# A new order of the steps of a one-core attention and long-convolution kernel on Trainium2

## The chip, the cores and the metric

The kernel runs on one core of one Trainium2 chip. The metric is device time in microseconds (us); the shown time of a kernel is the median of several executions. The engines are named as in the profile: PE (TensorE matmul) with PEld (its weight loads), DVE (VectorE), ACT (ScalarE), POOL (GpSimd) and SP (SyncE). Each engine works through its own instructions in program order and waits on semaphores for the others.

## The reference

```python
kv  = einsum('bhsd,bhse->bhde', k, v)           # (8, 8, 64, 64)
o   = einsum('bhsd,bhde->bhse', q, kv)          # (8, 8, 576, 64)
x   = o / sqrt(mean(o*o, -1) + 1e-6) * g_norm   # -> (8, 576, 512)
x1, x2, x3 = split(x @ w_proj, 3)               # each (8, 576, 512)
x2c = irfft(rfft(x2, n=576) * rfft(filter, n=576), n=576)   # along the sequence
out = (x1 * x2c * x3) @ w_out                   # (8, 576, 512), float32
```

Inputs are float32; the loads cast them to bf16.

## The kernel before

The eight batches (0 to 7) go one after the other through the same steps, and steps of two or three neighbouring batches are interleaved. The order of all 688 steps is written out by hand in one text, `ORDER`; a word `name.batch` calls the step of that name, and each call issues its instructions on their engines at once. So `ORDER` fixes the program of every engine, the queues of SP and POOL among them. A third field (`T0.0.20`) puts that many idle products (512 columns, line 100) on PE ahead of the step.

The steps that the text below speaks of, with their engine and line:

- Loads on POOL's queue: `Lq`, `Lk`, `Lv` (one batch of q, k, v; `a` and `b` are halves; line 121), `Lw1` to `Lw3` and `Lwo` (weights, line 130), `Lf` (the filter, line 294). q, k and v have two buffers each, so batch n+2 waits until batch n is used up. `Zi` and `Zd` make index tables and the identity on POOL, `Zp` clears a part of the folded filter on POOL (its tile lies where the angles of the tables lay).
- `Qt` (line 405) transposes q by a DMA on SP's queue for batches 2 to 7; `Qh` (line 409) is a tiny POOL copy that reads the result. For batches 0 and 1 `T0`, `T1` (PE) and `eTv`, `eTa` (DVE) do it.
- `K`, `Ka`, `Kb` (PE, line 380) and `eK` (ACT) make kv, `O01`, `O23` (PE, line 454) the attention output, `sq`, `ob` (ACT) or `ov` (DVE) read it, `R`, `rs` (PE line 461, ACT line 475) the norm, `x0`, `x1` (DVE, line 489) the normalised x of two head pairs each.
- `fd`, `fr`, `fa` (DVE, lines 500 to 514) fold x along the sequence; both operands of their instructions lie in SBUF, as those of `x0` and `x1`. `rrM`, `rrT`, `abM`, `abT` (PE, lines 530 to 550) multiply the folds with w2; ACT copies the results out (`err`, `eab`, `eT`).
- `F0`, `F1`, `F2` (PE) are the forward transform, `M0`, `M1` (DVE, line 602) the products with the filter's transform: PSUM to the float32 tile `tpw`, 97 or 128 rows of 2048. `A0`, `A1` (POOL, line 608) sum the halves of `tpw` into the bf16 tile `Y`; `Av` does the same on DVE. `M2` (DVE, line 617) needs no sum.
- `Ga`, `Gb` (PE, line 627) are the two gates, `x10` to `x13` (ACT) and `g0` to `g3` (DVE, line 635: one operand in PSUM, one in SBUF) read them.
- `Io`, `I` (PE, lines 654 and 655), `os` (ACT), `u`, `w`, `fin` (DVE) are the inverse transform and the gating; `U`, `ot` (PE line 750, ACT and SP) the last product and the store.
- `Tb0` to `Tb2`, `Ff0` to `Ff2`, `H0` to `H2` build the tables and the filter's transform once, at the start.

PSUM is four pairs of banks. `take` gives a step the pair that was freed longest ago in `ORDER`; PE then waits until the engine named by that freeing step has read it. The functions that the change touches, and what calls them:

Of the kernel before, what the change touches and what calls it, by code (L numbers as in the profile page):

```python
# [19 lines left out]
ORDER = """Z.0 Zi.0 Lg.0 Lkb.0 Zt.0 Lq.0 Lvb.0 Lva.0 An.0 Lka.0 Zd.0 Zf.0 Lf.0 Tg.0 Zp.0 T0.0.20 Act.0 eTv0.0 T1.0 Lw1.0 Kb.0  # L20
eKb.0 Tb2.0 eTv1.0 Tb1.0 Lq.1 Lw2.0 Tb0.0 O23.0 sq2.0 Ka.0 R2.0.1 sq3.0 eKa.0 ov2.0 O01.0 rs2.0 ov3.0 sq1.0 R3.0 ov1.0
sq0.0 R1.0.1 rs3.0 rs1.0 x1.0 R0.0 ov0.0 rs0.0 x0.0 Ff2.0 Ff0.0 fd0.0 Ff1.0 Ga0.0 fr0.0 fr1.0 Lw3.0 fa0.0 Ga1.0 x11.0
Lv.1 fd1.0 x10.0 H1.0 H0.0 rrM.0 Lk.1 fa1.0 T0.1 rrT.0 err.0 eTa0.1 H2.0 Gb1.0 HN0.0 HN1.0 abM.0 F0.0 Gb0.0 eab.0 g1.0
K.1 M0.0 T1.1 abT.0 Lk.2 g0.0 eK.1 O01.1 eTa1.1 eT.0 sq0.1 ob0.1 F2.0 F2t.0 M2.0 sq1.1 Ga2.0 Lv.2 Lq.2 x12.0 Gb2.0
ob1.1 R1.1 g2.0 rs1.1 F1.0 R0.1 F1t.0 O23.1 rs0.1 sq2.1 Ga3.0 ob2.1 sq3.1 M1.0 R2.1 rs2.1 x0.1 ob3.1 x13.0 Av1.0 A0.0
Gb3.0 g3.0 R3.1 rs3.1 Lq.3 Qt.2 K.2 eK.2 Io01.0 I01.0 x1.1 Ga1.1 fd.1 Ga0.1 os01.0 u01.0 x11.1 Io23.0 O01.2 fr.1 x10.1
os23.0 sq0.2 I23.0 sq1.2 rrM.1 Qh.2 ob0.2 u23.0 ob1.2 Qt.3 R0.2 fa.1 rs0.2 w.0 rrT.1 err.1 O23.2 fin.0 abM.1 sq2.2
ob2.2 F0.1 eab.1 sq3.2 abT.1 eT.1 Gb1.1 Gb0.1 ob3.2 F1.1 M0.1 g1.1 R2.2 F1t.1 Lv.3 g0.1 rs2.2 Lk.3 R3.2 Ga3.1 rs3.2
R1.2 x13.1 Lwo.0 K.3 Lk.4 rs1.2 M1.1 Gb3.1 A0.1 x1.2 F2.1 Lv.4 x0.2 eK.3 A1.1 O23.3 F2t.1 g3.1 sq3.3 sq2.3 M2.1 fd.2
fa.2 U0.0 Io01.1 ob3.3 ob2.3 os01.1 ot0.0 Ga2.1 I01.1 x12.1 Gb2.1 R3.3 Io23.1 u01.1 rs3.3 g2.1 os23.1 I23.1 O01.3  # L30
abM.2 Lq.4 u23.1 w.1 sq1.3 sq0.3 Qh.3 Lq.5 Ga0.2 fin.1 ob1.3 ob0.3 abT.2 eab.2 x10.2 Ga1.2 R1.3 eT.2 fr.2 R0.3 x11.2
Gb1.2 rs1.3 F1.2 R2.3 rs0.3 F1t.2 g1.2 rrM.2 rs2.3 F2.2 rrT.2 K.4 M1.2 Qt.4 Lk.6 F2t.2 U2.0 eK.4 Lv.6 Lk.5 Lv.5 err.2
x1.3 Ga3.2 x0.3 M2.2 O23.4 ot2.0 x13.2 F0.2 sq3.4 sq2.4 ob2.4 Lq.6 ob3.4 fr.3 U0.1 M0.2 Qt.5 Gb0.2 R2.4 g0.2 Gb3.2
ot0.1 rs2.4 A1.2 A0.2 R3.4 g3.2 rrM.3 rs3.4 Io01.2 rrT.3 I01.2 os01.2 err.3 I23.2 Ga2.2 Gb2.2 fd.3 x12.2 fa.3 u01.2
g2.2 Io23.2 os23.2 u23.2 abM.3 abT.3 U4.1 eab.3 Ga0.3 ot4.1 F1.3 eT.3 w.2 fin.2 x10.3 O01.4 sq1.4 ob1.4 Qh.4 F1t.3
M1.3 sq0.4 U2.1 Ga1.3 ob0.4 ot2.1 F0.3 K.5 x1.4 A1.3 x11.3 F2.3 Gb0.3 eK.5 F2t.3 M0.3 R0.4 g0.3 Ga2.3 rs0.4 x12.3 R1.4
Gb2.3 M2.3 O23.5 rs1.4 Gb1.3 g2.3 x0.4 sq3.5 A0.3 sq2.5 ob3.5 ob2.5 U0.2 Io01.3 I01.3 Qt.6 fd.4 g1.3 fa.4 Ga3.3 os01.3
Gb3.3 x13.3 u01.3 Io23.3 g3.3 fr.4 abT.4 ot0.2 O01.5 os23.3 I23.3 eT.4 sq0.5 ob0.5 u23.3 Lk.7 abM.4 sq1.5 K.6 ob1.5
w.3 Ga0.4 eab.4 F1.4 R2.5 eK.6 x10.4 F1t.4 rs2.5 R3.5 rs3.5 rrM.4 R0.5 rs0.5 F2.4 fin.3 M1.4 x1.5 rrT.4 F2t.4 err.4
Ga1.4 R1.5 Gb1.4 M2.4 x11.4 Lv.7 rs1.5 O23.6 g1.4 sq3.6 F0.4 U2.2 sq2.6 ob3.6 Qh.5 Ga3.4 M0.4 ob2.6 ot2.2 O01.6 x13.4  # L40
Gb3.4 sq1.6 x0.5 Gb0.4 ob1.6 A1.4 g3.4 sq0.6 R3.6 ob0.6 A0.4 rs3.6 g0.4 U4.3 Ga2.4 ot4.3 R2.6 Gb2.4 fr.5 x12.4 rs2.6
fd.5 Io01.4 R1.6 I01.4 g2.4 os01.4 rrM.5 Io23.4 rs1.6 rrT.5 u01.4 os23.4 err.5 K.7 x1.6 I23.4 R0.6 Zn.0 fa.5 u23.4
abM.5 abT.5 rs0.6 eK.7 eab.5 U2.3 Lq.7 F0.5 Ga0.5 Qt.7 ot2.3 w.4 F1.5 fin.4 eT.5 F2.5 x10.5 M0.5 A0.5 F1t.5 U0.4 x0.6
M1.5 ot0.4 F2t.5 M2.5 A1.5 U0.3 Gb0.5 ot0.3 O23.7 sq3.7 g0.5 Ga1.5 Gb1.5 ob3.7 x11.5 fd.6 Io01.5 Ga2.5 fa.6 sq2.7 g1.5
I01.5 ob2.7 Ga3.5 os01.5 Io23.5 fr.6 x12.5 x13.5 Gb3.5 u01.5 Gb2.5 I23.5 os23.5 g3.5 g2.5 abM.6 Ga0.6 u23.5 eab.6
x10.6 O01.7 sq0.7 abT.6 ob0.7 eT.6 sq1.7 w.5 rrM.6 ob1.7 F1.6 Qh.6 rrT.6 F2.6 F1t.6 fin.5 err.6 F2t.6 U0.5 M1.6 Ga1.6
A1.6 F0.6 ot0.5 R2.7 M2.6 R1.7 x11.6 rs2.7 Gb0.6 U4.5 rs1.7 M0.6 R0.7 Gb1.6 A0.6 ot4.5 g0.6 R3.7 rs0.7 Ga2.6 U2.4
rs3.7 g1.6 I01.6 x12.6 Io01.6 Gb2.6 ot2.4 x1.7 Ga3.6 x0.7 fr.7 os01.6 u01.6 g2.6 rrM.7 fd.7 fa.7 x13.6 Io23.6 I23.6
os23.6 Gb3.6 g3.6 rrT.7 Ga1.7 err.7 abM.7 x11.7 u23.6 eab.7 F0.7 Ga0.7 x10.7 abT.7 w.6 F1.7 M0.7 eT.7 fin.6 Gb0.7 g0.7
F1t.7 F2.7 Ga2.7 x12.7 A0.7 F2t.7 Gb1.7 M1.7 U2.5 Av1.7 Qh.7 M2.7 g1.7 U2.6 Gb2.7 vae0.6 Io01.7 vve1.6 I01.7 ot2.5  # L50
g2.7 dse0.6 Ga3.7 dge1.6 J3.7 os01.7 x13.7 uj3.7 J2.7 dge2.6 uj2.7 U0.6 Gb3.7 u01.7 w01.7 dae3.6 fin01.7 wo23.7 wm23.7
Vq0.7 ot0.6 U4a.7 g3.7 fo23.7 U4b.7 vau.7 fm23.7 dsu2.7 Vq2.7 Vp0.7 dgu1.7 vaq0.7 vvq1.7 dsu0.7 dgu3.7 Vp2.7 dgq1.7
dsq0.7 dsq2.7 vap0.7 daq3.7 vvp1.7 dgp3.7 dap1.7 dsp0.7 dgp2.7"""


@with_exitstack
def kernel(
# [249 lines left out]
    def fold_filter(a, ev):  # L307
        pp = take("ffp")
        for odd in range(2):
            for s in range(2):  # L310
# [2 lines left out]
        ev(out=tmp['ff'][:, a], in_=pp)
        free("ffp")

    @one
    def Ff2(b):
# [4 lines left out]
        for odd, ev in enumerate((vec.tensor_copy, act.copy)):
            ev(out=tmp['ff'][0:32, 2, odd], in_=pp[32 * odd:32 * odd + 32])
# [554 lines left out]
```

## Time and profile before

| | |
|---|---|
| median of 3 runs | 218.24 us (218.19 to 220.13) |
| profiled execution | 219.81 us |
| its span, first to last instruction | 218.0 us |
| mean granted TensorE clock | 0.987 |
| busy: PE, DVE, ACT, POOL | 200.0, 184.0, 147.4, 68.1 us |

The profiled execution took 1.8 us more than its span and 1.6 us more than the median. In the lists of instructions, the columns are the start in us from the span's begin, the duration in us, engine, line, operation, tiles, shapes and the count of merged instructions; in brackets stands the idle time of the engine just before, and what ended it. A merged row's duration runs from the first start to the last end. In the table by stretches, each engine has its busy us and its instruction count.

### The profile page before, as it was taken

The numbers are of one execution on the slowest core, as the hardware profiler recorded it, in microseconds if no ns is written. First come the engines' busy times: TensorE is split into PE (matmuls) and PEld (weight loads), VectorE is DVE, ScalarE is ACT, GpSimd is POOL, SyncE is SP. The second block draws the span as 40 slices with busy tenths as digits, with TensorE's granted clock in tenths as the row PEclk, the third lists the DMA queues.
The fourth block names the chain that finished last, engine by engine and source line by source line (L and its number), as shares of the span: only waits on it lengthen the run. The fifth ranks groups of instructions, "written<-read, shape, count | busy, mean of one in ns | idle before, by whom it ended". The sixth has DMA issues, their size and how long they took to land.

```text
span 218.0 us, 4583 instructions
## 1 busy us (share of the span) xinstructions
PE 200.0 (92%) x1825; PEld 123.2 (57%) x1848; DVE 184.0 (84%) x275; ACT 147.4 (68%) x232; POOL 68.1 (31%) x67
## 2 busy tenths in 40 slices
PE   4978899898999999599999999999999999999960
...
PEclk9999999999999999799999999999999999999998
...
GB/s 64 203 208 206 205 204 203 187 182 163 205 174 146 230 86 146 230 156 191 240 147 188 121 0 98 154 115 96 164 32 0 38 111 96 0 3 18 178 205 132
DMA packets 40810, 30.12 MB, mean 138 GB/s; under 512 B 15796, under 2 KB 36276, under 8 KB 40788
## 3 DMA queue, kind: packets, MB, share of 16 engines
...
q14 instruction: 8, 0.07, 0.1%
...
## 4 chain that ended last, share of the span: by engine, by line
PE 69%; DVE 15%; DMA 5%; issue 3%; ACT 3%; POOL 1%; POOLq 0%; DVEq 0%; ACTq 0%
PE ps L627 24%; PE ps L750 10%; PE ps L544 5%; DMA wp<-in_moe_w_proj_dram 5%; DVE tpw L602 4%; PE ps L654 4%; PE ps L530 3%; PE ps L550 3%; PE ps L461 3%; PE ps L380 2%; PE ps L537 2%; PE ps L454 2%; PE ps L763 1%; PE ps L569 1%; PE ps L576 1%
## 5 line engine op out<-in xcount | busy, mean ns | idle before, releaser
L627 PE MATMUL ps<-x,wp 128*128 128x288 bf16 x512 | 72.5, 288 | 2.9 <-DVE tpw L602 2.4
L608 POOL TENSOR_TENSOR Y<-tpw 97x1024 bf16<-97x1024 f32 (+1 forms) x14 | 36.9, 2638 | 100.9 <-DVE tpw L602 100.8
L627 PEld LDWEIGHTS <-wp 128*128 128x128 bf16 x512 | 48.9, 98 | 21.5 <-issue 6.0
L602 DVE TENSOR_TENSOR tpw<-ps,HH 97x2048 f32<-97x2048 f32 (+1 forms) x16 | 36.6, 2288 | 3.6 <-PE ps L583 1.9
L635 DVE TENSOR_TENSOR g<-ps,x 128x576 bf16<-128x576 f32 x32 | 24.0, 753 | 8.3 <-PE ps L627 6.5
L475 ACT ACTIVATE rstd<-ps,bias_eps 128x576 bf16<-128x576 f32 x32 | 23.1, 748 | 7.5 <-PE ps L461 7.5
L633 ACT CAST x<-ps 128x576 bf16<-128x576 f32 x32 | 20.5, 644 | 10.9 <-PE ps L627 10.4
L750 PE MATMUL ps<-wo,yg 128*128 128x512 bf16 x106 | 26.0, 379 | 0.6 <-DVE g L635 0.2
L554 ACT CAST x<-ps 128x1024 bf16<-128x1024 f32 (+1 forms) x24 | 21.0, 874 | 8.2 <-PE ps L544 5.2
L464 ACT ACTIVATE sq<-ps 128x576 bf16<-128x576 f32 x32 | 20.1, 657 | 1.8 <-PE ps L454 1.6
L471 ACT ACTIVATE o<-ps,g_col 128x576 bf16<-128x576 f32 x28 | 20.3, 753 | 0.0
L754 ACT COPY ot<-ps 128x1024 f32<-128x1024 f32 x13 | 13.2, 1018 | 7.9 <-PE ps L750 7.8
L750 PEld LDWEIGHTS <-yg 128*128 128x128 bf16 x112 | 10.7, 98 | 12.1 <-issue 0.5
L654 PE MATMUL ps<-IV,Y 128*128 128x192 bf16 x120 | 15.6, 246 | 0.0
L544 PE MATMUL ps<-wp,ab 128*128 128x512 bf16 x58 | 14.8, 379 | 0.4
L663 DVE TENSOR_TENSOR u<-ps,os 128x576 bf16<-128x576 f32 x15 | 11.3, 754 | 3.1 <-ACT os L658 1.5
L461 PE MATMUL ps<-sq,ind 128*128 128x288 bf16 x64 | 13.0, 291 | 0.9 <-DVE o L469 0.5
L658 ACT COPY os<-ps 128x576 f32<-128x576 f32 x15 | 9.6, 642 | 5.5 <-PE ps L655 3.8
L655 PE MATMUL ps<-IV,Y 97*128 97x96 bf16 x60 | 12.4, 207 | 0.0
L489 DVE TENSOR_TENSOR x<-o,rstd 128x1152 bf16<-128x1152 bf16 x16 | 11.8, 750 | 0.7 <-ACT rstd L475 0.6
L386 ACT CAST kvblk<-ps 64x256 bf16<-64x256 f32 (+2 forms) x25 | 8.8, 353 | 4.5 <-PE ps L380 4.3
L654 PEld LDWEIGHTS <-Y 128*128 128x128 bf16 x120 | 9.6, 98 | 3.3 <-issue 1.1
...
## 6 DMA issues: line engine op xcount, KB each, us to landing
...
qb<-in_q_dram POOLq DMA_DIRECT2D x8, 576.0 KB, 8.7
vb<-in_v_dram POOLq DMA_DIRECT2D x7, 576.0 KB, 10.7
kb<-in_k_dram POOLq DMA_DIRECT2D x7, 576.0 KB, 12.2
wp<-in_moe_w_proj_dram POOLq DMA_DIRECT2D x3, 512.0 KB, 11.4
...
```

The source lines that it names most:

```text
L464: act.activation(out=halves(sq()[:, j]), in_=tmp['o', b, j][:, :, 0:TH], func=AF.Square)
L471: act.activation(out=by_time(osb(), j), in_=i_, func=AF.Copy, scale=g_col)
L475: act.activation(out=by_time(rstd(), j), in_=by_row(tmp['r', b, j]), func=AF.Abs_reciprocal_sqrt, scale=1.0 / D, bias=bias_eps)
L544: nc.tensor.matmul(pp[:, h], abt()[:, j, 2 * h * P:(2 * h + 1) * P], w2(j), start=(j == 0), stop=(j == NDC - 1))
L554: act.copy(out=o_(), in_=tmp[key, b])
L602: vec.tensor_mul(out=t_[:n], in0=xp[:n].unsqueeze(1).to_broadcast([n, 2, 2, DM]), in1=two)
L608: op(out=Yt()[:n, 2 * g:2 * g + 2], in0=t_[:n, ::-1, 0], in1=t_[:n, ::-1, 1])
L627: nc.tensor.matmul(pp[:, h, 0:TH], w_, x[:, j, h * TH:(h + 1) * TH], start=(j == 0), stop=(j == NDC - 1))
L633: act.copy(out=x1, in_=pp[:, :, 0:TH])
L635: vec.tensor_mul(out=halves(g13t()[:, dc]), in0=pp[:, :, 0:TH], in1=x1)
L654: nc.tensor.matmul(pp[:, i, 0:SB], Y[:, 2 * g + h, cs], IV[:, 2 * g + h, 0:SB], start=(g == 1), stop=(g == 2))
L750: nc.tensor.matmul(pp[:, cc], ygt(b)[:, dc, b % 2 * 64 + c * P:b % 2 * 64 + (c + 1) * P], wo[:, dc], start=(dc == 0), stop=(dc == NDC - 1))
```

## The change

`ORDER` is a new sequence of the same 688 steps; no step is added or dropped. The idle products ahead of `T0.0` become 22 (from 20), the one ahead of `R1.0` goes, the one ahead of `R2.0` stays. The tile of the folded filter is made by whichever step comes first (`ffb`), which issues no other instruction.

POOL's queue at the start and up to batch 7's loads, before and after (from `ORDER`):

```text
before: Zi Lkb.0 Lq.0 Lvb.0 Lva.0 Lka.0 Zd Lf Zp Lw1 Lq.1 Lw2 Lw3 Lv.1 Lk.1 Lk.2 Lv.2 Lq.2 A0.0 Lq.3 Qh.2
  Lv.3 Lk.3 Lwo Lk.4 A0.1 Lv.4 A1.1 Lq.4 Qh.3 Lq.5 Lk.6 Lv.6 Lk.5 Lv.5 Lq.6 A1.2 A0.2 Qh.4 A1.3 A0.3 Lk.7
  Lv.7 Qh.5 A1.4 A0.4 Lq.7 A0.5 A1.5 Qh.6 A1.6 A0.6 A0.7 Qh.7
after:  Zi Zd Lq.0 Lkb.0 Lvb.0 Lva.0 Lka.0 Lf Lq.1 Lw1 Lw2 Zp Lw3 Lk.1 Lv.1 Lv.2 Lk.2 Lq.2 A0.0 Lq.3 Qh.2
  Lk.3 Lv.3 Lwo A0.1 Lq.4 Lk.4 A1.1 Lv.4 Qh.3 A1.2 Lk.5 Lk.6 A0.2 Lq.5 Lv.5 Qh.4 A1.3 Lv.6 A0.3 Lq.6 Qh.5
  A1.4 A0.4 Lq.7 Lv.7 Lk.7 A0.5 A1.5 Qh.6 A1.6 A0.6 A0.7 ... Qh.7
```

The diff, with `ORDER` cut to the places that matter:

```diff
-ORDER = """Z.0 Zi.0 Lg.0 Lkb.0 Zt.0 Lq.0 Lvb.0 Lva.0 An.0 Lka.0 Zd.0 Zf.0 Lf.0 Tg.0 Zp.0 T0.0.20 Act.0 eTv0.0 T1.0 Lw1.0 Kb.0
-eKb.0 Tb2.0 eTv1.0 Tb1.0 Lq.1 Lw2.0 Tb0.0 O23.0 sq2.0 Ka.0 R2.0.1 sq3.0 eKa.0 ov2.0 O01.0 rs2.0 ov3.0 sq1.0 R3.0 ov1.0
-sq0.0 R1.0.1 rs3.0 rs1.0 x1.0 R0.0 ov0.0 rs0.0 x0.0 Ff2.0 Ff0.0 fd0.0 Ff1.0 Ga0.0 fr0.0 fr1.0 Lw3.0 fa0.0 Ga1.0 x11.0
...
-Gb1.2 rs1.3 F1.2 R2.3 rs0.3 F1t.2 g1.2 rrM.2 rs2.3 F2.2 rrT.2 K.4 M1.2 Qt.4 Lk.6 F2t.2 U2.0 eK.4 Lv.6 Lk.5 Lv.5 err.2
-x1.3 Ga3.2 x0.3 M2.2 O23.4 ot2.0 x13.2 F0.2 sq3.4 sq2.4 ob2.4 Lq.6 ob3.4 fr.3 U0.1 M0.2 Qt.5 Gb0.2 R2.4 g0.2 Gb3.2
-ot0.1 rs2.4 A1.2 A0.2 R3.4 g3.2 rrM.3 rs3.4 Io01.2 rrT.3 I01.2 os01.2 err.3 I23.2 Ga2.2 Gb2.2 fd.3 x12.2 fa.3 u01.2
...
+ORDER = """Zi.0 Z.0 Zd.0 Lg.0 Zt.0 An.0 Tg.0 Lq.0 Lkb.0 Zf.0 Act.0 T0.0.22 eTv0.0 Lvb.0 T1.0 Lva.0 Lka.0 Kb.0 eTv1.0 eKb.0 Tb1.0
+Tb0.0 Lf.0 Lq.1 O23.0 Lw1.0 sq2.0 Ka.0 Lw2.0 R2.0.1 sq3.0 eKa.0 ov3.0 Zp.0 Lw3.0 rs2.0 R3.0 ov2.0 Lk.1 O01.0 rs3.0
+sq1.0 sq0.0 x1.0 ov1.0 ov0.0 Ff0.0 Ff2.0 R1.0 rs1.0 R0.0 rs0.0 x0.0 Ff1.0 Tb2.0 T1.1 T0.1 eTa1.1 Ga0.0 fr0.0 fr1.0
...
+eab.2 rrM.2 rs1.3 F1.2 R2.3 F1t.2 g1.2 rrT.2 rs2.3 F2.2 err.2 x0.3 Qh.3 K.4 Qt.4 eK.4 F2t.2 M1.2 A1.2 U2.0 x1.3 M2.2
+Ga3.2 O23.4 ot2.0 x13.2 sq3.4 fr.3 Lk.5 F0.2 U0.1 sq2.4 ob3.4 Gb3.2 ob2.4 Gb0.2 Lk.6 M0.2 A0.2 fd.3 ot0.1 rrM.3 R2.4
+rrT.3 g0.2 Ga2.2 g3.2 rs2.4 R3.4 err.3 Io01.2 x12.2 I01.2 os01.2 rs3.4 U4.1 Io23.2 fa.3 Gb2.2 u01.2 os23.2 I23.2 abM.3
+Lq.5 ot4.1 abT.3 g2.2 x1.4 u23.2 eab.3 w.2 Ga0.3 eT.3 F1.3 O01.4 F1t.3 x10.3 U2.1 Qt.5 sq1.4 ob1.4 sq0.4 M1.3 Lv.5
+Ga1.3 ob0.4 fin.2 ot2.1 F0.3 R0.4 x11.3 rs0.4 Qh.4 K.5 eK.5 F2.3 M0.3 A1.3 Gb0.3 R1.4 g0.3 F2t.3 M2.3 rs1.4 Ga2.3
+x12.3 Gb2.3 O23.5 g2.3 sq3.5 ob3.5 Gb1.3 x0.4 Lv.6 A0.3 Ga3.3 g1.3 Io01.3 sq2.5 Lq.6 ob2.5 os01.3 x13.3 I01.3 fd.4
...
+    def ffb():
+        if 'ff' not in tmp:
+            tmp['ff'] = work.tile([P, 3, 2, DM], BF16, name="ff", tag="tpw1")
+        return tmp['ff']
+
     @one
     def Zp(b):
-        tmp['ff'] = work.tile([P, 3, 2, DM], BF16, name="ff", tag="tpw1")
-        nc.gpsimd.memset(tmp['ff'][:, 2], 0.0)
+        nc.gpsimd.memset(ffb()[:, 2], 0.0)
...
-        ev(out=tmp['ff'][:, a], in_=pp)
+        ev(out=ffb()[:, a], in_=pp)
...
-        ff = tmp['ff']
+        ff = ffb()
```

More of the change, by code (lines that the diff above doesn't have):

```diff
@@ L17 @@
 MAGIC = 3.0 * (2.0 ** 22)
-ORDER = """Z.0 Zi.0 Lg.0 Lkb.0 Zt.0 Lq.0 Lvb.0 Lva.0 An.0 Lka.0 Zd.0 Zf.0 Lf.0 Tg.0 Zp.0 T0.0.20 Act.0 eTv0.0 T1.0 Lw1.0 Kb.0
-eKb.0 Tb2.0 eTv1.0 Tb1.0 Lq.1 Lw2.0 Tb0.0 O23.0 sq2.0 Ka.0 R2.0.1 sq3.0 eKa.0 ov2.0 O01.0 rs2.0 ov3.0 sq1.0 R3.0 ov1.0
-sq0.0 R1.0.1 rs3.0 rs1.0 x1.0 R0.0 ov0.0 rs0.0 x0.0 Ff2.0 Ff0.0 fd0.0 Ff1.0 Ga0.0 fr0.0 fr1.0 Lw3.0 fa0.0 Ga1.0 x11.0
-Lv.1 fd1.0 x10.0 H1.0 H0.0 rrM.0 Lk.1 fa1.0 T0.1 rrT.0 err.0 eTa0.1 H2.0 Gb1.0 HN0.0 HN1.0 abM.0 F0.0 Gb0.0 eab.0 g1.0
@@ L24 @@
[L24 to L28, printed above, removed]
@@ L29 @@
-R1.2 x13.1 Lwo.0 K.3 Lk.4 rs1.2 M1.1 Gb3.1 A0.1 x1.2 F2.1 Lv.4 x0.2 eK.3 A1.1 O23.3 F2t.1 g3.1 sq3.3 sq2.3 M2.1 fd.2
-fa.2 U0.0 Io01.1 ob3.3 ob2.3 os01.1 ot0.0 Ga2.1 I01.1 x12.1 Gb2.1 R3.3 Io23.1 u01.1 rs3.3 g2.1 os23.1 I23.1 O01.3
-abM.2 Lq.4 u23.1 w.1 sq1.3 sq0.3 Qh.3 Lq.5 Ga0.2 fin.1 ob1.3 ob0.3 abT.2 eab.2 x10.2 Ga1.2 R1.3 eT.2 fr.2 R0.3 x11.2
-Gb1.2 rs1.3 F1.2 R2.3 rs0.3 F1t.2 g1.2 rrM.2 rs2.3 F2.2 rrT.2 K.4 M1.2 Qt.4 Lk.6 F2t.2 U2.0 eK.4 Lv.6 Lk.5 Lv.5 err.2
-x1.3 Ga3.2 x0.3 M2.2 O23.4 ot2.0 x13.2 F0.2 sq3.4 sq2.4 ob2.4 Lq.6 ob3.4 fr.3 U0.1 M0.2 Qt.5 Gb0.2 R2.4 g0.2 Gb3.2
@@ L34 @@
-ot0.1 rs2.4 A1.2 A0.2 R3.4 g3.2 rrM.3 rs3.4 Io01.2 rrT.3 I01.2 os01.2 err.3 I23.2 Ga2.2 Gb2.2 fd.3 x12.2 fa.3 u01.2
[L35 to L53, printed above, removed]
+ORDER = """Zi.0 Z.0 Zd.0 Lg.0 Zt.0 An.0 Tg.0 Lq.0 Lkb.0 Zf.0 Act.0 T0.0.22 eTv0.0 Lvb.0 T1.0 Lva.0 Lka.0 Kb.0 eTv1.0 eKb.0 Tb1.0
@@ new lines @@
+Tb0.0 Lf.0 Lq.1 O23.0 Lw1.0 sq2.0 Ka.0 Lw2.0 R2.0.1 sq3.0 eKa.0 ov3.0 Zp.0 Lw3.0 rs2.0 R3.0 ov2.0 Lk.1 O01.0 rs3.0
+sq1.0 sq0.0 x1.0 ov1.0 ov0.0 Ff0.0 Ff2.0 R1.0 rs1.0 R0.0 rs0.0 x0.0 Ff1.0 Tb2.0 T1.1 T0.1 eTa1.1 Ga0.0 fr0.0 fr1.0
+x10.0 eTa0.1 H0.0 H1.0 rrM.0 HN0.0 H2.0 rrT.0 Gb0.0 err.0 Gb1.0 fd0.0 g0.0 Ga1.0 fd1.0 F0.0 Lv.1 Lv.2 fa0.0 fa1.0 Lk.2
+Ga2.0 Lq.2 HN1.0 x11.0 K.1 x12.0 g1.0 M0.0 abM.0 abT.0 eK.1 eab.0 O01.1 eT.0 F2.0 sq0.1 A0.0 F2t.0 Gb2.0 ob0.1 M2.0
+sq1.1 F1.0 Lq.3 R1.1 g2.0 ob1.1 F1t.0 R0.1 rs1.1 rs0.1 Qt.2 M1.0 O23.1 Av1.0 sq2.1 ob2.1 sq3.1 Ga3.0 Gb3.0 x13.0 R2.1
@@ new lines @@
+ob3.1 Io01.0 R3.1 g3.0 x0.1 I01.0 rs2.1 K.2 rs3.1 os01.0 x1.1 eK.2 Io23.0 u01.0 fr.1 Ga0.1 os23.0 Ga1.1 x10.1 O01.2
+x11.1 fd.1 sq0.2 sq1.2 I23.0 ob1.2 fa.1 ob0.2 Qt.3 rrM.1 rrT.1 Qh.2 u23.0 abT.1 R0.2 Lk.3 w.0 err.1 eT.1 O23.2 rs0.2
+F0.1 sq2.2 sq3.2 ob3.2 abM.1 ob2.2 M0.1 Lv.3 Gb1.1 eab.1 R3.2 fin.0 R2.2 rs3.2 rs2.2 Gb0.1 F1.1 g1.1 Lwo.0 g0.1 R1.2
+F1t.1 A0.1 Ga3.1 rs1.2 M1.1 K.3 Gb3.1 x13.1 x1.2 eK.3 F2.1 O23.3 g3.1 F2t.1 Lq.4 sq3.3 Lk.4 M2.1 A1.1 sq2.3 U0.0
+Io01.1 ob3.3 I01.1 x0.2 ob2.3 os01.1 ot0.0 Ga2.1 Io23.1 fd.2 x12.1 Ga1.2 u01.1 os23.1 fa.2 x11.2 I23.1 R3.3 Gb2.1
```

19 lines of the change are left out of this document (18 added, 1 removed).

## The prediction

> **What bounds the kernel now.** I read the page's slices first, then the table by stretches around the one odd slice, then the chain and the engines' lists there. From the page:
>
> ```profile
> PE   4978899898999999599999999999999999999960
> PEclk9999999999999999799999999999999999999998
> ```
>
> PE is full in nearly every slice after the start. One slice, the seventeenth (from about 87 us), is half empty, and the clock dips there. By stretches:
>
> ```profile
> core 0: us, PE busy (x) PEld busy (x) DVE busy (x) ACT busy (x) POOL busy (x), PEclk, DMA share, GB/s
> 46.00:84.40 38.40, 36.76 (x371) 23.04 (x373) 36.66 (x48) 31.72 (x54) 15.36 (x17) 1.00 1.07 170
> 84.40:89.50 5.10, 2.98 (x19) 1.73 (x18) 5.10 (x4) 3.54 (x6) 2.33 (x2) 1.00 1.20 205
> 89.64:93.05 3.41, 3.19 (x13) 1.83 (x13) 2.03 (x4) 0.74 (x1) 2.28 (x2) 0.50 1.26 213
> 93.05:198.70 105.65, 104.96 (x898) 65.58 (x910) 93.99 (x113) 70.62 (x108) 27.45 (x15) 1.00 0.53 100
> ```
>
> From 46 to 84.4 PE and DVE share the bound (1.6 and 1.7 us idle of 38.4). From 93 to 199 PE alone is the bound: 0.7 us idle of 105.65, so no order can win there more than that. Between lie 2.12 us of idle PE and 3.41 us at a granted clock of 0.50. The chain says what PE waited for:
>
> ```profile
> 84.43 2.40 issue
> 86.84 0.35 DVE rr L509
> 87.18 2.21 DVE tpw L602
> 89.44 1.92 PE ps L627 x8
> ```
>
> The gate on PE waits for `M0.2` to free its PSUM pair, `M0.2` waits in DVE's queue behind `fr.3`, and `fr.3` stands for 2.40 us in which no semaphore was missing. DVE, then POOL, then PE in that place:
>
> ```profile
> 77.81 2.29 DVE L602 TENSOR_TENSOR tpw<-ps,HH 128x2048 f32<-128x2048 f32 x1
> 80.02 1.42 DVE L489 TENSOR_TENSOR x<-o,rstd 128x1152 bf16<-128x1152 bf16 x2
> 81.36 1.22 DVE L617 TENSOR_TENSOR Y<-ps,HM 128x1024 bf16<-128x1024 f32 x1
> 82.49 0.55 DVE L505 TENSOR_TENSOR x<-x 128x768 bf16<-128x768 bf16 x1
> 83.07 0.56 DVE L507 TENSOR_TENSOR x<-x,x 128x768 bf16<-128x768 bf16 x1
> 83.67 3.52 DVE L509 TENSOR_TENSOR rr<-x 128x384 bf16<-128x384 bf16 x2
> 87.10 2.28 DVE L602 TENSOR_TENSOR tpw<-ps,HH 97x2048 f32<-97x2048 f32 x1
> ...
> 82.79 0.77 POOL L121 DMA_DIRECT2D vb<-in_v_dram  x1
> 83.55 0.77 POOL L121 DMA_DIRECT2D qb<-in_q_dram  x1
> 84.33 2.36 POOL L608 TENSOR_TENSOR Y<-tpw 128x1024 bf16<-128x1024 f32 x1
> ...
> 84.21 1.89 PE L750 MATMUL ps<-wo,yg 128*128 128x512 bf16 x8
> 85.93 1.14 PE L627 MATMUL ps<-x,wp 128*128 128x288 bf16 x8
> 86.91 0.41 PE L461 MATMUL ps<-sq,ind 128*128 128x288 bf16 x2
> 89.44 1.92 PE L627 MATMUL ps<-x,wp 128*128 128x288 bf16 x8 [2.12 <-DVE tpw L602]
> ...
> L509 DVE TENSOR_TENSOR rr<-x x18: 249/351/3245, 22.6 to 180.7; 128x384 bf16<-128x384 bf16 x14, 128x192 bf16<-128x192 bf16 x4
> ```
>
> The first half of line 509 takes 3.25 us against a median of 0.35: 2.9 us lost, and it ends (86.9) with POOL's sum (84.33 + 2.36 = 86.7). It began at 83.67, ahead of the sum but behind the issue of `Lq.6` (83.55), on whose heels the sum followed without a gap. Line 507 ran at its usual length beside the issue before that one, so an issue alone does not hold DVE. `A1.2` had stood ready since `M1.2` ended at 80.1, behind five issues.
>
> The Trainium skill, "SBUF — State Buffer", section "SBUF: two separate sides", has VectorE and GpSimd share one port pair as an exclusive lock, won by whichever starts first. The trace agrees that a two-input DVE operation and a sum exclude each other, but not on who wins: here the one that started 0.66 us earlier lost.
>
> **The change, part by part.** *The hold.* In the new queue `A1.2` stands behind `Qh.3` and ahead of `Lk.5` and `Lk.6`; `Lv.6`, `Lv.5`, `Lq.6` move far behind. So nothing of `fr.3` falls behind an issue with a ready sum. What comes instead is the sum itself, right behind `M1.2`. How that goes:
>
> ```profile
> 62.15 3.47 POOL L608 TENSOR_TENSOR Y<-tpw 128x1024 bf16<-128x1024 f32 x1 [0.42 <-DVE tpw L602]
> ...
> 61.98 1.42 DVE L489 TENSOR_TENSOR x<-o,rstd 128x1152 bf16<-128x1152 bf16 x2
> 63.32 0.75 DVE L635 TENSOR_TENSOR g<-ps,x 128x576 bf16<-128x576 f32 x1
> ```
>
> DVE's two-input operations that stand directly behind the product go first (the sum is 1.1 us longer than the 2.36 above), and operations with one input in PSUM run beside a sum. The new DVE order is `x0.3 M1.2 x1.3 M2.2 fr.3 M0.2`. By the durations above: `x0.3` (0.71) now precedes `M1.2`, which ends at 80.8; `x1.3` to 81.5; the sum 81.5 to 83.85; beside it `M2.2` to 82.7; `fr.3` is held 1.15 us, to 83.85, then needs 0.55 + 0.56 + 2 x 0.35 = 1.8 to 85.65, `M0.2` 2.29 to 87.9. On PE, `Gb3.2` and `Gb0.2` (0.98 each) now both stand behind `U0.1`, from 85.93 to 87.9, and only then comes `rrM.3`, whose pair `M0.2` frees. So PE's wait falls from 2.12 to about 0: **-2.1**. If the sum did not hold `fr.3`, nothing more would be won, since PE is busy till 87.9; if `fr.3` were held the full 2.4 us, 1.2 would be lost again.
>
> *The clock.* Half speed for 3.41 us, with PE busy 3.19 of it, costs 1.6 to 1.7 us. It begins 0.2 us after the wait's end; a wait gone takes it along: **-1.7**, or 0 if something else brought it.
>
> The Trainium skill, "TensorE: Matmul & The Clock Gate", Part 1, "HAM oscillation", warns of idle gaps above some 3.4 us. Here 2.12 us sufficed, so the row is worse than the page; taken strictly, the page would leave the dip to another cause and the sum at 2.1 less.
>
> *The start.* POOL makes the identity first and loads q before k; `Zp` moves behind `Lw2`; `q.1` is loaded ahead of `Lw1`, and `T1.1`, `T0.1` and `Tb2` move up before `Ga0.0`; PE's work up to `K.1` stays the same but for an `abM` against a `Ga2` and a `T1`.
>
> ```profile
> 10.00:15.00 5.00, 4.26 (x100) 3.33 (x96) 3.54 (x11) 4.93 (x11) 4.16 (x6) 1.00 1.22 218
> 15.00:20.00 5.00, 3.77 (x38) 1.79 (x39) 4.12 (x7) 4.71 (x9) 2.93 (x5) 1.00 1.22 196
> 20.00:25.00 5.00, 4.41 (x44) 2.46 (x38) 4.76 (x15) 3.46 (x5) 0.74 (x1) 1.00 1.26 207
> ...
> 21.51 0.58 ACT L323 CAST ff<-ps 32x512 bf16<-32x512 f32 x1 [1.74 <-DVE ff L323]
> 22.11 1.93 ACT L313 CAST ff<-ps 128x1024 bf16<-128x1024 f32 x2
> ```
>
> ACT bounds the stretch from 10 to 20 (4.93 and 4.71 of 5). Two more idle products cost 2 x 0.24 (eight of that width in 1.89), one fewer gives 0.24 back: +0.24. ACT now casts `Ff0` (0.97) and `Ff2` (0.58) ahead of `rs1` and `rs0`, so `x0.0` and the first gate come 1.5 us later; the q transposes that PE meets there (0.6 each) fill most of it. I take **+0.5** together. Bounds: PE idles 0.74 + 1.23 + 0.59 = 2.56 in these rows, the most that a better start can win; the other end is 1.5 + 0.24 = +1.7 without the filling. The value lies near the loss end, since ACT's row is the fuller one.
>
> *The loads.* They now come later.
>
> ```profile
> qb<-in_q_dram POOLq DMA_DIRECT2D x8, 576.0 KB, 8.7
> ...
> DMA to landing us min/median/max: 18.3/18.3/18.3
> ...
> 106.52 0.95 PE L380 MATMUL ps<-vb,kb 96*64 96x64 bf16 x48
> ...
> DMA to landing us min/median/max: 6.3/6.3/6.3
> ...
> 135.48 0.79 POOL L121 DMA_DIRECT2D qb<-in_q_dram  x1
> 149.18 0.38 PE L576 MATMUL ps<-x,FY 128*128 128x512 bf16 x1
> ```
>
> These are the size of a load, `Lv.5`'s time to landing, the start of `K.5`, then `Lq.7`'s time to landing and issue, and the end of `F1.5`. The times below are on the old clock, without the start's 0.5. `Lv.5` landed at 82.8 + 18.3 = 101.1, 5.4 us before its use. Now it waits behind `A0.2`, which follows `M0.2` (87.9), `fd.3` (0.95) and lasts 2.36: `Lq.5` at 91.2, `Lv.5` at 92.0. An uncontended load lands after 6.3 us, and one behind it 2.9 later (576 KB at 205 GB/s): 100.4; at the pace of the crowded one (four such behind each other, 18.3 / 4 = 4.6) 104. `K.5` would come at 106.5 - 3.8 + 0.4 (`R0.4` ahead) = 103.1: from 2.7 early to 0.9 late. `K.7` now stands behind `F1.5`, with one gate more and itself less ahead of it: 149.6 - 3.8 = 145.8. Its `Lk.7` is third behind `A0.4` (135.5 - 3.8 = 131.7) and lands at 131.7 + 6.3 = 138.0 plus twice 2.9 to 4.6, 143.8 to 147.2: 2.0 early to 1.4 late. I take 0 for both, at most +2.3.
>
> *The rest.* `Qh.7` moves to the last stores, into POOL's waits there. SP's `Qt.5` goes behind `ot0.1` and `ot4.1`, after `Lq.5`. Elsewhere the order shifts a step or two among neighbours with equal PE work; 0.7 us is the most to win after 93, 1.6 between 46 and 84.
>
> Sum: -2.1 - 1.7 + 0.5 = **-3.3**: from the profiled execution's 219.8 to 216.5, its span from 218.0 to 214.7. That execution lay 1.6 above the median of 218.24, so I take the difference to the median: **214.9**.
>
> **Rivals.** *Late loads.* The wait goes, but `K.5` or `K.7` waits for its load: for it speaks the slack, down from 5.4 us to about none, against it that the DMA engines are less crowded from 93 on (share 0.53). All of +2.3: 217.2.
>
> *Late loads with the clock: slower.* `K.5` waits for v.5, because `Lq.5`, two stores and `Qt.5` share the engines with it. A wait of 2.1 us was enough to halve the clock; from there a wait of L costs L + 1.7. It decides at L = 1.6 to 2.1, where the gain of 3.3 is used up. At twice the crowded pace, v.5 lands at 92.0 + 6.3 + 2 x 4.6 = 107.5, L = 4.4: 214.9 + 6.1 = 221.0.
>
> *The clock dip stays* for another cause: 218.24 - 2.1 + 0.5 = 216.6.
>
> *The hold only moves.* `Lv.6` now stands directly ahead of `A0.3`, with `A0.3` ready when it is issued: the same picture. DVE then has `g0.3 M2.3 g2.3` (0.75 + 1.22 + 0.75 = 2.7), all with an operand in PSUM, before `x0.4`; issue and sum last 0.77 + 2.36 = 3.1, so 0.4 is held if PSUM work passes, 3.1 if not. The 63.32 row speaks for passing. If not, 218.
>
> *More than that:* the start gains its 1 and the middle 1: 213.
>
> **How the numbers follow.** Forecast 214.9 with 0.58 (own range 213.8 to 216.0); late loads 0.16; the dip stays 0.06; the hold moves 0.07; slower 0.08; more 0.05. The range of 8 in 10 runs from 213.2 to 217.8: it leaves out the slower rival and the tails. One per cent is 2.2 us and about what a measurement of this kernel tells from no change: below 216.06 lie the forecast but for its upper edge, "more" and a part of the late loads, 0.64; within 1% the rest of these and the moved hold, 0.28; slower 0.08.
>
> **What would show it.** No line 509 above 0.6 us; `fr.3`'s first instruction about 1.1 us longer than its 0.55; no PE wait on line 602 near 88; a 9 in every slice of the granted clock but the last; `K.1` within 1 us of its place. Wrong it would be made by a PE wait at `K.5` or `K.7` on a load, by another two-input DVE operation that lasts over 2 us, or by a first gate after 24 us.

## The result, and the profile after

The changed kernel took **217.39 us** (median of 20 executions, 216.30 to 220.70), the kernel before beside it 219.57 us (20 executions, 218.19 to 221.12). The ratio is 0.9914 with a 95% interval of 0.9888 to 0.9940; it compares means, without the changed kernel's two executions of 220.03 and 220.70 us, which count as slow. So the change is 0.9% less: the interval excludes a ratio of 1, but the gain stays under the one per cent that the forecast took as what a measurement of this kernel tells from no change. The time lies in the range of the forecast and 2.5 us above its value. A later set of the changed kernel gave 218.30 us (12 executions) and a ratio of 0.9936 (0.9903 to 0.9970).

The median of before moves between sets (218.24, 218.37, 219.05, 219.57, 219.82 us) because its executions fall into two groups, called the lower and the upper below: 8 of the 20 lay at 218.19 to 218.31 us, 10 at 219.43 to 219.85. The profiled execution of before (219.81) is of the upper group, the median of 218.24 that the forecast started from is of the lower.

Of the changed kernel an execution of the later set is read (217.68 us, span 215.9), since the first profiled one (220.70, span 218.9) ran a part of its start at half clock, that is at a granted clock of 0.50; that one is shown for the start and for its wait at `K.5`. The page's slices:

```profile
PE   4978999999999999999699999999999999999960
PEclk9999999999999999999999999999999999999996
```

The half empty slice at 87 us and the dip of the clock (3.41 us at 0.50) are gone. A new notch, a 6, stands in the twentieth slice, from 102.6 us. By stretches (busy us of each engine, then granted clock, DMA share and GB/s):

```profile
core 0: us, PE busy (x) PEld busy (x) DVE busy (x) ACT busy (x) POOL busy (x), PEclk, DMA share, GB/s
84.40:89.50 5.10, 5.05 (x33) 2.85 (x33) 5.07 (x7) 2.99 (x5) 2.65 (x3) 1.00 1.04 160
89.64:93.05 3.41, 3.41 (x35) 2.68 (x33) 3.03 (x5) 2.85 (x5) 2.68 (x4) 1.00 1.20 247
93.05:102.60 9.55, 9.50 (x67) 5.32 (x66) 8.60 (x11) 7.13 (x11) 1.21 (x1) 1.00 1.14 198
102.60:106.40 3.80, 2.18 (x60) 1.71 (x60) 2.18 (x1) 1.87 (x5) 3.79 (x3) 1.00 1.02 158
106.40:196.60 90.20, 89.41 (x736) 55.58 (x747) 81.70 (x100) 60.23 (x91) 24.19 (x14) 1.00 0.50 100
```

PE, idle for 2.12 of the 5.10 us from 84.4 before, is idle for 0.05, and the 3.41 us behind it run at full clock. The new idle time, 1.62 us, stands between 102.6 and 106.4. DVE, then POOL, then PE around the place of the old hold:

```profile
78.51 2.29 DVE L606 TENSOR_TENSOR tpw<-ps,HH 128x2048 f32<-128x2048 f32 x1
80.72 0.75 DVE L493 TENSOR_TENSOR x<-o,rstd 128x1152 bf16<-128x1152 bf16 x1
81.39 1.22 DVE L621 TENSOR_TENSOR Y<-ps,HM 128x1024 bf16<-128x1024 f32 x1
82.52 1.59 DVE L509 TENSOR_TENSOR x<-x 128x768 bf16<-128x768 bf16 x1
84.14 0.56 DVE L511 TENSOR_TENSOR x<-x,x 128x768 bf16<-128x768 bf16 x1
84.73 0.63 DVE L513 TENSOR_TENSOR rr<-x 128x384 bf16<-128x384 bf16 x2
85.28 2.28 DVE L606 TENSOR_TENSOR tpw<-ps,HH 97x2048 f32<-97x2048 f32 x1
...
80.88 2.81 POOL L612 TENSOR_TENSOR Y<-tpw 128x1024 bf16<-128x1024 f32 x1 [13.57 <-DVE tpw L606]
83.63 1.56 POOL L121 DMA_DIRECT2D kb<-in_k_dram  x2
...
85.66 2.12 PE L631 MATMUL ps<-x,wp 128*128 128x288 bf16 x16
87.62 1.03 PE L534 MATMUL ps<-wp,rr 128*128 128x512 bf16 x3
```

(The changed file's lines are 4 higher: old 505, 507, 509 are now 509, 511, 513; old 602 and 608 are 606 and 612.) The sum runs behind `M1.2`. `x1.3`, which began 0.16 us ahead of it, keeps its 0.75 (the sum lasts 2.81 instead of 2.36); `M2.2` with its PSUM operand keeps 1.22; `fr.3`'s first fold, begun at 82.52, takes 1.59 instead of 0.55 and ends 0.4 after the sum. The long first half of the old line 509 is gone, `M0.2` ends at 87.56, and PE goes from the gates to `rrM.3` without a wait.

What came instead stands in the chain of waits:

```profile
90.58 0.79 POOL qb L121
91.37 12.72 DMA vb<-in_v_dram
104.09 0.14 issue
104.23 0.95 PE ps L384 x48
```

`K.5` waits for v.5, issued at 91.37 and landed 12.72 us later.

### The profile page after: what moved, and what is told of

It is laid out like the page before. It is cut to its first block, busy times and chain, and to the rows that moved or that the text cites. A ratio compares the mean times of both kernels' runs of the same rounds, so it can differ in the third digit from the quotient of the medians.

```text
span 218.9 us, 4602 instructions
## 1 busy us (share of the span) xinstructions
PE 202.4 (92%) x1849; PEld 122.5 (56%) x1849; DVE 182.8 (84%) x275; ACT 148.1 (68%) x232; POOL 70.8 (32%) x67
## 4 chain that ended last, share of the span: by engine, by line
PE 69%; DMA 12%; DVE 7%; ACT 5%; POOL 3%; issue 2%; POOLq 0%; DVEq 0%; ACTq 0%
PE ps L631 24%; PE ps L754 9%; DMA vb<-in_v_dram 6%; PE ps L548 6%; DMA fn<-in_moe_filter_fft_dram 6%; PE ps L658 4%; DVE tpw L606 3%; PE ps L465 3%; PE ps L554 2%; PE ps L309 2%; PE ps L384 2%; PE ps L534 2%; PE ps L458 2%; PE ps L580 1%; PE ps L793 1%
## 5 line engine op out<-in xcount | busy, mean ns | idle before, releaser
L612 POOL TENSOR_TENSOR Y<-tpw 97x1024 bf16<-97x1024 f32 (+1 forms) x14 | 38.8, 2770 | 112.4 <-DVE tpw L606 112.3
L631 PE MATMUL ps<-x,wp 128*128 128x288 bf16 x512 | 71.3, 286 | 0.8 <-ACT rstd L479 0.3
L637 ACT CAST x<-ps 128x576 bf16<-128x576 f32 x32 | 20.5, 644 | 10.6 <-PE ps L631 10.5
L558 ACT CAST x<-ps 128x1024 bf16<-128x1024 f32 (+1 forms) x24 | 20.4, 881 | 6.8 <-PE ps L548 3.3
L754 PEld LDWEIGHTS <-yg 128*128 128x128 bf16 x112 | 10.6, 98 | 11.6 <-issue 0.5
L621 DVE TENSOR_TENSOR Y<-ps,HM 128x1024 bf16<-128x1024 f32 x8 | 9.7, 1218 | 2.2 <-PE ps L598 2.2
```

The lines of the kernel that those rows point to most:

```text
L612: op(out=Yt()[:n, 2 * g:2 * g + 2], in0=t_[:n, ::-1, 0], in1=t_[:n, ::-1, 1])
L631: nc.tensor.matmul(pp[:, h, 0:TH], w_, x[:, j, h * TH:(h + 1) * TH], start=(j == 0), stop=(j == NDC - 1))
L637: act.copy(out=x1, in_=pp[:, :, 0:TH])
L754: nc.tensor.matmul(pp[:, cc], ygt(b)[:, dc, b % 2 * 64 + c * P:b % 2 * 64 + (c + 1) * P], wo[:, dc], start=(dc == 0), stop=(dc == NDC - 1))
```

## The experiments

Each edit is in `ORDER`; the lines of code stay those of the kernel it starts from. The two theories at the outset: the time before was lost to a sum directly behind an issue, and given back by a load that is now late; or the order gains nothing there and the difference between the two kernels is one of the clock.

**Before, with the sum behind `M1.2`.**

```diff
-M1.2 Qt.4 Lk.6 F2t.2 U2.0 eK.4 Lv.6 Lk.5 Lv.5 err.2 x1.3 Ga3.2 x0.3 ... ot0.1 rs2.4 A1.2 A0.2
+M1.2 A1.2 Qt.4 F2t.2 U2.0 eK.4 Lk.5 Lv.5 Lk.6 Lv.6 err.2 x1.3 Ga3.2 x0.3 ... ot0.1 rs2.4 A0.2
```

> The kernel before with A1.2 moved directly behind M1.2, ahead of the five loads (and k.5, v.5 issued ahead of k.6, v.6, so that K.5 does not wait for its load). Nothing else moves. If the hold from the issue on is what cost the time: no line-509 instruction of 3.2 us; instead the first fold of fr.3 (line 505) about 1.0 us longer than its 0.55; PE's 2.1 us wait for M0.2 down to 1.0 or less; granted clock 1.00 from 86 to 94; 2.5 to 3.8 us less than the kernel before. Rival (any sum costs DVE the same, wherever it stands): the wait on M0.2 stays at 2 us and the time within 0.5 us of before.

Measured: 217.57 us (217.48 to 217.68), ratio 0.9929 (0.9904 to 0.9954): 1.5 us less than before, where at least 2.5 was expected. DVE, then POOL in this kernel:

```profile
80.04 3.58 DVE L489 TENSOR_TENSOR x<-o,rstd 128x1152 bf16<-128x1152 bf16 x2
83.54 1.21 DVE L617 TENSOR_TENSOR Y<-ps,HM 128x1024 bf16<-128x1024 f32 x1
84.67 0.54 DVE L505 TENSOR_TENSOR x<-x 128x768 bf16<-128x768 bf16 x1
...
80.20 2.79 POOL L608 TENSOR_TENSOR Y<-tpw 128x1024 bf16<-128x1024 f32 x1 [12.95 <-DVE tpw L602]
82.95 0.79 POOL L121 DMA_DIRECT2D kb<-in_k_dram  x1
```

Line 509 is at its usual length, and the five issues from 82.95 on, with no sum behind them, hold nothing. But here two `x` follow the product, and the second, begun at 80.70, after the sum, is held until the sum ends: the pair takes 3.58 us instead of 1.42, and PE waits 1.3 us for `M2.2`. So the long operation is the sum's doing wherever it stands; the place decides which DVE step pays.

**The same, with `x0.3` ahead of `M1.2`**, as the changed kernel has it.

```diff
-K.4 M1.2 A1.2 ... x1.3 Ga3.2 x0.3 M2.2
+K.4 x0.3 M1.2 A1.2 ... x1.3 Ga3.2 M2.2
```

> The first experiment (the kernel before with A1.2 behind M1.2) with x0.3 moved ahead of M1.2 as well. If the sum's own lock is what is left there: no line-489 instruction of 2.9 us; the first fold of fr.3 lasts 1.6 instead of 0.55; PE's waits of 1.3 and 0.3 us there gone; 1.0 to 1.6 us less than that first experiment, about 216.2. Rival (PE is bound by something else there): within 0.4 us of it.

Measured: 216.74 us (216.19 to 218.70, six executions), ratio 0.9884 (0.9843 to 0.9925), 0.8 us less than the first experiment, where 1.0 to 1.6 was expected.

```profile
83.70 1.58 DVE L505 TENSOR_TENSOR x<-x 128x768 bf16<-128x768 bf16 x1
```

The held `x` is gone, and `fr.3`'s fold pays 1.03 us, as in the changed kernel. The profiled execution (217.65) also has a wait of 1.8 us for a q transposition near 49 us, which the edits don't touch. These two edits of before, without any other part of the new order, are at least as good as all of it.

**Before, with one issue less ahead of the sum.**

```diff
-sq3.4 sq2.4 ob2.4 Lq.6 ob3.4 fr.3 ... A1.2 A0.2
+sq3.4 sq2.4 ob2.4 ob3.4 fr.3 ... A1.2 A0.2 Lq.6
```

> The kernel before with Lq.6 moved behind A0.2, so that A1.2 stands directly behind Lv.5's issue (82.8 to 83.55). If the issue ahead of a ready sum already takes the ports: the instruction of line 507 that starts at 83.07, inside that issue, is the long one (2.8 to 2.9 us instead of 0.56) and line 509 is normal. Rival (whoever starts first has the ports): line 507 lasts 0.56, the sum begins late or is longer, and the first instruction of line 509 takes about 2.6 us.

Measured: 219.42 us (218.06 to 219.71), ratio 0.9982 (0.9946 to 1.0019). DVE, then POOL:

```profile
82.63 0.55 DVE L505 TENSOR_TENSOR x<-x 128x768 bf16<-128x768 bf16 x1
83.21 3.28 DVE L507 TENSOR_TENSOR x<-x,x 128x768 bf16<-128x768 bf16 x1
86.53 0.63 DVE L509 TENSOR_TENSOR rr<-x 128x384 bf16<-128x384 bf16 x2
...
82.92 0.77 POOL L121 DMA_DIRECT2D vb<-in_v_dram  x1
83.70 2.36 POOL L608 TENSOR_TENSOR Y<-tpw 128x1024 bf16<-128x1024 f32 x1
```

The sum now follows `Lv.5`, and the long operation moves one instruction forward: line 507 takes 3.28 us instead of 0.56, having begun 0.49 us ahead of the sum but 0.29 behind the issue; line 509 is normal. This is the hold as the prediction read it: from an issue with a ready sum directly behind it, to the sum's end. Whether the issue does it, or the sum takes the ports earlier than its recorded start, the rows don't tell.

The Trainium skill, "SBUF — State Buffer", section "SBUF: two separate sides", gives the lock to whichever engine starts first. `x1.3` above, begun 0.16 us ahead of a sum with no issue before it, agrees; this row, and the row of line 509 in the kernel before, don't: there an issue stands directly ahead of the sum.

**Before, with idle products in PE's wait**: they end no wait of DVE or POOL, they only keep PE busy.

```diff
-Qt.5 Gb0.2 R2.4 g0.2 Gb3.2
+Qt.5 Gb0.2 R2.4.8 g0.2 Gb3.2
```

> The kernel before with eight idle products (1.7 us of PE) ahead of R2.4, inside PE's 2.1 us wait for M0.2; the wait's end is unchanged. If the wait itself halves the clock for the 3.41 us behind it: granted clock 1.00 there and 1.5 to 1.7 us less. Rival (the dip has another cause): the 3.41 us at 0.50 stay and the time is within 0.3 us of before.

Measured: 218.34 us (218.10 to 218.78), ratio 0.9959 (0.9930 to 0.9988). The stretches, then PE:

```profile
84.40:89.50 5.10, 4.71 (x28) 2.47 (x26) 5.10 (x4) 3.16 (x6) 2.33 (x1) 1.00 1.21 211
89.64:93.05 3.41, 3.38 (x27) 1.93 (x26) 2.81 (x4) 1.70 (x4) 3.08 (x2) 1.00 1.25 211
...
86.95 1.89 PE L100 MATMUL ps<-kvblk,ind 128*128 128x512 bf16 x8
89.48 1.14 PE L627 MATMUL ps<-x,wp 128*128 128x288 bf16 x8 [0.39 <-DVE tpw L602]
```

The hold stays (line 509: 3.25 us) and PE is released at the same time, but the clock stays at 1.00 and all twelve executions lie at or near the lower group of before. So the idle 2.12 us brought the half clock, and the half clock is the 1.5 us between the groups. Which group an execution falls into changes with the same program: in the sets beside the experiments, 31 of 69 executions of before took less than 218.4 us, with a mean granted clock of 0.988 to 0.996, and 35 took 219.6 or more, with 0.980 to 0.988. The mean clock alone doesn't place an execution: in the first experiment, 0.982 and 0.995 went with 217.52 and 217.60 us.

**The changed kernel, with v.5 loaded earlier.**

```diff
-fr.3 Lk.5 F0.2 ... M1.3 Lv.5 Ga1.3
+fr.3 Lk.5 Lv.5 F0.2 ... M1.3 Ga1.3
```

> The kernel after with Lv.5 moved up from behind A0.2 and Lq.5 to directly behind Lk.5. If the late v.5 costs its whole wait: PE's 2.16 us wait before K.5 gone (v.5 lands before 101 us), 1.8 to 2.2 us less than after, that is 3.8 to 4.3 less than before. Rival (the wait only moves, to O23.5 for q.5's transposes, which then land later, or to DVE): less than 1 us won against after.

Measured: 224.23 us (223.77 to 226.30, six executions), ratio 1.0242 (1.0194 to 1.0290): 2.4% more than before. `K.5` no longer waits, but `O23.5` waits for the q transposition. The issue of `Lq.5` (its time to landing), SP's `Qt.5`, and PE's `O23.5`:

```profile
L121 POOL DMA_DIRECT2D qb<-in_q_dram x1: 803/803/803, 93.1 to 93.1; - x1
DMA to landing us min/median/max: 13.2/13.2/13.2
...
106.44 3.04 SPq L409 DMA_TRANSPOSE qT<-qb  x1
...
115.78 0.69 PE L458 MATMUL ps<-qT,kvblk 64*64 64x288 bf16 x8 [5.95 <-DMA qT<-qb]
```

With v.5 ahead of it, q.5 lands at 106.3, 2.2 us later than in the first profiled execution of the changed kernel, where it was issued at the same time (93.0) and landed at 104.1. `Qt.5` can only start then, and lands after 9.3 us instead of 6.5. PE waits 5.95 us, and from 112.5 to 119.3 the granted clock is 0.50, half of that behind the wait. So a load that is moved ahead pushes back the next one. (This execution, 226.30 us, had a half clock in its start as well; the other five took 223.77 to 224.26.)

**The changed kernel, with q.5 and v.5 loaded earlier**, q.5 as before directly behind `Qh.3`.

```diff
-x0.3 Qh.3 K.4 ... fr.3 Lk.5 F0.2 ... abM.3 Lq.5 ot4.1 ... M1.3 Lv.5
+x0.3 Qh.3 Lq.5 K.4 ... fr.3 Lk.5 Lv.5 F0.2 ... abM.3 ot4.1 ... M1.3
```

> The kernel after with Lq.5 issued ahead of A1.2 (behind Qh.3) and Lv.5 directly behind Lk.5, so that neither stands behind A0.2. If the late loads of batch 5 are what eats the gain: no PE wait at K.5 (2.2 us in after) nor at O23.5 (6.0 us with v.5 alone moved), 1.5 to 2.3 us less than after. Rival (the DMA engines are the bound there, so that another load or transposes come late): within 0.7 us of after, with a PE wait of over 1 us on a DMA between 80 and 115 us.

Measured: **216.31 us** (216.04 to 216.50, six executions), ratio 0.9849 (0.9816 to 0.9881): the lowest median of all. PE waits nowhere more than 0.3 us between 20 and 200. The same kernel shows the place at which the hold might have moved, `Lv.6` directly ahead of `A0.3`, whose input `M0.3` is done at 105.10, just behind the issue's start; POOL, then DVE:

```profile
105.07 0.79 POOL L121 DMA_DIRECT2D vb<-in_v_dram  x1
105.87 2.36 POOL L612 TENSOR_TENSOR Y<-tpw 97x1024 bf16<-97x1024 f32 x1
...
105.21 0.76 DVE L639 TENSOR_TENSOR g<-ps,x 128x576 bf16<-128x576 f32 x1
105.88 1.21 DVE L621 TENSOR_TENSOR Y<-ps,HM 128x1024 bf16<-128x1024 f32 x1
```

Both operations, one begun behind the issue and one beside the sum, keep their usual length: work with an operand in PSUM passes. (In the changed kernel itself the product at 106.57 takes 0.76 beside that sum, which runs from 105.55 to 107.91.) No DVE operation with both operands in SBUF stands there, so the rows don't show what would happen to one.

**The changed kernel, with q.5 alone earlier**, to tell the queue's length from the time of `Lv.5`'s issue.

```diff
-x0.3 Qh.3 K.4 ... abM.3 Lq.5 ot4.1
+x0.3 Qh.3 Lq.5 K.4 ... abM.3 ot4.1
```

> The changed kernel with only Lq.5 moved, from ahead of Qt.5 to behind Qh.3; Lv.5 stays behind the q transposition's issue. Theory (K.5 waits because v.5 shares the engines with q.5, the output stores and Qt.5): v.5 lands after 6.3 to 10 us instead of 12.7 to 13.3, about 98 to 102, K.5 does not wait, and the time is that of the version with both moved, 216.3. Rival (v.5 is late because it is issued at 91 to 94, whatever stands ahead of it): K.5 waits 0.5 us or more and the time is 217 or above.

Measured: 216.36 us (216.01 to 216.72, six executions), ratio 0.9891 (0.9857 to 0.9926). `Lv.5`, then PE's `K.5`:

```profile
L121 POOL DMA_DIRECT2D vb<-in_v_dram x1: 803/803/803, 91.1 to 91.1; - x1
DMA to landing us min/median/max: 9.6/9.6/9.6
...
103.01 0.95 PE L384 MATMUL ps<-vb,kb 96*64 96x64 bf16 x48
```

`Lv.5` is issued at 91.1 as in the changed kernel (91.4), lands after 9.6 us instead of 12.7, and `K.5` doesn't wait. So what made it late is q.5 ahead of it, not the hour of its issue. One moved load recovers all that the two did (the times compare better than the ratios here: before had a median of 219.82 us beside the one and 218.37 beside the other).

**The changed kernel behind the start of before.** `ORDER` of before up to `K.1`, of after from there.

> The order of the kernel before up to K.1, and from there on the remaining steps in the order of after. If the new start loses time (filter landing 1.3 us later behind which q.1 and w1 are in flight, PE waiting on it, the clock halved from 17 to 24 us): 1 to 2.5 us less than after, no half clock between 10 and 30 us. Rival (the start is a draw and the half clock there is this one execution's): within 0.5 us of after.

Measured: 219.05 us (218.64 to 223.07), ratio 1.0007 (0.9979 to 1.0036): neither less than the changed kernel nor close to it. It settles little: `K.1` comes at 34.2, but the seam adds delays of its own (`Qt.2` lands after 10.5 us, PE waits 1.3 us for it, `K.4` comes at 81.6 instead of 79.0).

**Idle products ahead of the filter's first product**, in the changed kernel and in the version with q.5 and v.5 early.

```diff
-ov0.0 Ff0.0 Ff2.0
+ov0.0 Ff0.0.6 Ff2.0
```

In the changed kernel:

> The changed kernel with the same six idle products ahead of Ff0 and nothing else. Theory: its upper executions (219 to 220.7) go, what is left is 217.0 to 218.8 with the 1.6 to 2.2 us that K.5 waits for v.5; K.1 at 34.2 to 35.3 and no half clock before 25 us. Rival: the spread from 216.3 to 220.7 stays, because it comes from how late v.5 lands and not from the start.

In the version with both loads early:

> The version with q.5 and v.5 loaded early (216.31 us), and six idle products (0.22 us each) ahead of the first filter product Ff0 on PE, where two profiled executions of the changed kernel's start waited 1.36 and 1.58 us for the filter and then ran 6.83 us at half clock. Theory (the wait for the filter makes the start's half clock): no execution has half clock before 25 us, all lie within 0.5 us of each other, and K.1 starts at 34.2 to 35.3, so 216.3 to 217.4. Rival (the half clock in the start is a draw that no product prevents): the spread of the changed kernel, over 2 us, shows here too in a window before 25 us.

Measured: 217.69 us (216.64 to 219.19) and 216.82 us (216.35 to 217.42), ratios 0.9939 (0.9904 to 0.9973) and 0.9901 (0.9866 to 0.9936). Neither profiled execution has a half clock before 25 us. The products cost 0.5 us in the better version (`K.1` at 35.2 instead of 34.3), whose executions spread over 1.1 us, more than the 0.5 of the theory. In the changed kernel one of twelve executions lies above 219 us, against six of the 32 without the products: too few to tell theory and rival apart. The profiled one waits 0.6 us for v.5, where two others of this kernel waited 1.6 and 2.2, so a part of the spread comes from there.

## Why the prediction was right and wrong

**The hold: right.** The forecast had `fr.3` held by 1.15 us and PE's wait of 2.12 gone. The fold took 1.59 instead of 0.55 (+1.04), `M0.2` ended at 87.56 against the 87.9 of the forecast, and PE's wait went. (The sum began at 80.88, ahead of the 81.5 of the forecast, and was the longer for it.) The size is best read without the clock: from before without the dip (218.34 with idle products, 218.2 to 218.3 for its lower group) to the order without late loads (216.31 and 216.36) it is 2.0 us, all that the new order does elsewhere included; the forecast had 2.1.

**The clock: the right mechanism, booked twice.** The half clock came from the wait, as said, and went with it; 1.5 us against 1.7. But only about half of the executions have it. The step that failed is the last one of the sum, "I take the difference to the median". The sum of -3.3 was made against an execution with the dip and held there: 219.8 - 3.3 = 216.5, and the versions without late loads have 216.40 and 216.50 in their profiled executions. The 1.6 us between that execution and the median of 218.24 was this same dip, absent in the median. Taken off again, it made 214.9. The forecast's own rival, "the clock dip stays", had 216.6 by the sum that was due for that median, for another reason.

**The loads: the term that was mis-sized.** The forecast bounded `K.5` by 2.7 us early to 0.9 late and took 0. PE was there at 102.6 instead of 103.1, v.5 landed at 104.1, and the wait was 1.6 us in the execution shown and 2.2 in the first one. What was wrong is the 6.3 us to landing for q.5, the time of a load with none ahead of it: `Lk.6`, issued at 84.4, was still landing until 97.5 when `Lq.5` was issued at 90.6, so q.5 took 10.6 us (landed 101.2); v.5 came 2.9 us behind it, the spacing that the forecast had. The late bound of 104 fits the landing by luck, since the terms given beside it make 102.1 (91.2 + 6.3 + 4.6), ahead of PE. And the share of 0.53 that spoke against late loads is a mean over 105 us: in before it was 1.31 from 93.05 to 102.6 and 0.32 from 120 on. `K.7` waited for nothing.

The rival "late loads" had this wait, and its time of 217.2 is close to the measured one by luck: it added 2.3 us to a 214.9 that was 1.6 too low. Of the 2.5 us that the forecast missed, 1.6 are the dip counted twice. The other 0.9 fit `K.5`'s wait, which was 0.6 to 2.2 us in the profiled executions; the two versions without it took 1.0 less than the changed kernel (216.31 and 216.36 against 217.39). The other rival of a late v.5, in which its wait halves the clock again, did not come: the first profiled execution waited 2.16 us, and the 3.41 us behind that ran at 1.00.

```profile
107.23 0.95 PE L384 MATMUL ps<-vb,kb 96*64 96x64 bf16 x48 [2.16 <-DMA vb<-in_v_dram]
```

**The start: +0.5 forecast, 0.0 to +2.5 seen.** PE's `K.1` in before, then in the changed kernel's execution read above, then in its first profiled one with the wait for the filter and the stretch behind it:

```profile
34.22 0.95 PE L380 MATMUL ps<-vb,kb 96*64 96x64 bf16 x48
...
34.21 0.95 PE L384 MATMUL ps<-vb,kb 96*64 96x64 bf16 x48
...
17.98 0.62 PE L309 MATMUL ps<-fn,ident 96*32 96x512 bf16 x4 [1.36 <-DMA fn<-in_moe_filter_fft_dram]
36.69 0.95 PE L384 MATMUL ps<-vb,kb 96*64 96x64 bf16 x48
...
16.90:23.73 6.83, 5.75 (x44) 2.13 (x44) 3.07 (x5) 4.07 (x7) 1.54 (x2) 0.50 1.27 206
```

The later set was run to see whether the half clock is the rule of the new start (`K.1` at 36.7 again) or comes in some executions only (`K.1` at 34 to 35.5, 216.5 to 217.5 us): its profiled execution had full clock there and `K.1` at 34.21, but took 217.68 us. The casts of `Ff0` and `Ff2` ahead of the norms cost nothing in it. In the first profiled execution the first gate comes at 25.15, one of the forecast's own signs of being wrong, as PE's wait at `K.5` was. What the forecast didn't have: `Ff0` now stands some 2 us earlier on PE and needs the filter at about 16.5, where it lands between 16.4 and 18.1. Whether that wait brings the half clock in the start isn't settled, since the version with q.5 alone early has the half clock without the wait:

```profile
13.30:16.70 3.40, 2.28 (x45) 1.15 (x45) 2.71 (x8) 3.34 (x7) 1.28 (x2) 0.99 1.03 198
...
16.70:20.10 3.40, 3.40 (x24) 1.17 (x24) 2.80 (x4) 2.28 (x4) 0.77 (x1) 0.50 1.29 204
```

There `K.1` came 0.5 us later and the whole took 216.50. PE was busy for 2.28 of the 3.40 us ahead of it; before was busy for 2.22 of the same stretch and kept its clock. What decides it stays open.

**The moved hold: refuted** for the PSUM work that stands there, by the rows of `Lv.6` and `A0.3` above.
